# New places for gate row tiles and w_mod tiles, two loads sooner, and an uneven last zero fill

## The chip, the cores and the metric

The kernel runs on one core of a Trainium2 chip. The metric is the device time of one execution in microseconds (us). A core has five engines with instruction streams of their own: TensorE (PE), VectorE (DVE), ScalarE (ACT), GpSimd (POOL) and SyncE (SP). Sixteen transfer engines move data between HBM and the on-chip memory, and from HBM to HBM; transfers are issued from GpSimd's queue (q0 in the profile) and from SyncE's (q1).

## The reference

The kernel computes one block (adaptive layer norm, attention of one query row over a window of the cache, gated feed-forward) forward and all its gradients. What matters here:

```python
mod = (silu(c) @ w_mod).reshape(1, 6, 1, -1)
sa, ca, ga, sb, cb, gb = (mod[:, i] for i in range(6))
h = layernorm(x) * (1 + ca) + sa
x = x + ga * A(h, k_cache, v_cache, wq, wo)   # the last 4096 of 65536 cache rows, 4 heads of keys
h = layernorm(x) * (1 + cb) + sb
x = x + gb * B(h, w_gate, w_up, w_down)       # (sigmoid(h @ w_gate) * (h @ w_up)) @ w_down
return x, *vjp(grad_out)   # gradients for x, k_cache, v_cache, wq, wo, w_gate, w_up, w_down, c, w_mod
```

The gradients of the two caches have 65536 rows for each of 4 heads, and only the last 4096 are not zero. The other 61440 rows of each are written as zeros: 120 fills of 1 MB. The gradients of the weights are outer products of a column and a row, since there is one token.

## The kernel before, in words

On chip there is one large tile, `arena`, of 192 places of 1 KB in each of 128 partitions. `ar(off, size)` is a piece of it, and every weight, tile and gradient has a place there for some time. The order of all work is written out by hand. Whoever writes into a place waits until the transfer out of it, or the reading of it, is over.

The zero fills are cut from a list, `zleft`; `zero(n)` (L185) takes the next n of it and issues them on GpSimd's queue. Most are one transfer: 128 rows of 8 KB, from an on-chip tile of zeros of one byte each that are widened on the way (L209), or 32 rows from HBM to HBM (L203). Six are narrow (L191 to L199): after a reset of a cursor a transfer of 5 rows of two 256-byte pieces (L194), then one of 60 rows of two 8-KB pieces (L197). `uneven` (L171) is a third kind, for fills whose number is in `UNEVEN` (L39). `UNEVEN` is empty, so that no fill takes it. The last fill, number 119, is the one of `zero(Z_ROWS[1])` (L1332).

The last quarter of the program makes weight gradients and stores them. Its helpers:

- `dwo(u)` (L1262): 1 MB of wo's gradient, four products on VectorE, one store.
- `dw_rows(k, j, off, outer)` (L1127): one 7-KB row tile (896 KB) of the gradient of w_up (k = 0) or w_gate (k = 1), at place `off`: one product on VectorE, one store on GpSimd's queue (L1130).
- `sec(j)` (L1256): a w_mod tile. A reduction (`ttr`) in place over `w5`, a part of w_mod that is `g_t[j]` for j < 6 and a fresh load in the tile's own last quarter for j = 6 and 7; then a product into `sec_t[j]` (8 KB) and its store (L1260). `g_t[3]` lies at 54, `g_t[0]` to `g_t[5]` at 48 to 58.
- `sec_load(j)` (L1253): that load for j = 6 and 7, 256 KB each, into the last 2 KB of `sec_t[j]`, at 54 and 62.
- `dwq_tile(j)` (L1306) and `s2(j)` (L1310): tiles of 8 KB and 4 KB of the gradients of wq and of w_mod's first third, one product and one store each.
- `grad_kv` (L1289): 32 blocks for the gradient of v (into `dv_home`, places 64 to 96), later for that of k (`dk_home`, 96 to 128): a matmul for each, then ScalarE, or ScalarE and VectorE in turn, copy it out. `dv_between` and `dk_between` put `sec`, `dwq_tile` and `s2` in among the blocks. `kv_store` (L1303) stores one head, 1 MB.

Lists give the places: `sec_t` (L1246), `dwq_t` (L1248), `s2_t` (L1249). Places 0 to 16 hold `w2_t` until the product `dcs234` (L1380), 128 to 144 hold `w01_T` until `dcs01` (L1440). The name `tail` (L1464) is SyncE's queue. GpSimd's transfers use eight semaphores in turn; one is issued when the one eight before it has landed.

Of the kernel before, what the change touches and what calls it, by code (L numbers as in the profile page):

```python
# [35 lines left out]
KIB = 512  # L36
SKIP = 4
NARROW = (15, 45, 75, 93, 103, 113)
UNEVEN = ()  # L39

def spread(total, n):
# [20 lines left out]
def kernel(  # L63
# [26 lines left out]
    nc = tc.nc  # L90
# [13 lines left out]
    def ar(off, size):  # L104
        return arena[:, int(off * KIB):int((off + size) * KIB)]

    def vt(shape, name, dt=FP32):
        return pool.tile(shape, dt, name=name)
# [4 lines left out]
    ZW = 4096  # L114
    zeros = vt([P, ZW // 2], "zeros", FP8)
# [55 lines left out]
    def uneven(piece):  # L171
        parts, at = [], 0
        flat_f = piece.rearrange("i x -> (i x)").bitcast(FP32)
        nc.gpsimd.inc_swdge_sem([], [], mode="reset_dge_cursor")
        for n, x in ((7, 16), (34, 512), (6, 16), (68, 512)):
            parts.append(nc.gpsimd.dma_start(
                out=flat_f[at:at + 2 * n * x].rearrange("(t p x) -> p t x", t=2, p=n),
                in_=zeros[0:n, 0:x].rearrange("p (t x) -> p t x", t=1).broadcast_to([n, 2, x])))
            at += 2 * n * x
        left = P * ZW // 2 - at  # L180
        nc.gpsimd.dma_start(out=flat_f[at:].rearrange("(p x) -> p x", p=16),
                            in_=zero_src.rearrange("i x -> (i x)")[0:left // 2].bitcast(FP8).rearrange("(p x) -> p x", p=16))
        return parts[0]

    def zero(n, after=None, big=False):  # L185
        for _ in range(n):
            if len(zleft) <= keep[0]:
                return
            region, narrow_ = zleft.pop(0)
            first = None  # L190
            if narrow_:  # L191
                nc.gpsimd.inc_swdge_sem([], [], mode="reset_dge_cursor")
                n = nlen - ncount.pop()
                first = nc.gpsimd.dma_start(  # L194
                    out=rest[0:NS, 0:nlen * 128].rearrange("p (t x) -> p t x", t=2)[:, :, n * 64:(n + 1) * 64],
                    in_=zeros[0:NS, 0:64].rearrange("p (t x) -> p t x", t=1).broadcast_to([NS, 2, 64]))
                ins = nc.gpsimd.dma_start(  # L197
                    out=region[8:P, :].bitcast(FP32).rearrange("(t p) x -> p t x", t=2),
                    in_=zeros[0:60, :].rearrange("p (t x) -> p t x", t=1).broadcast_to([60, 2, ZW // 2]))  # L199
            elif 119 - len(zleft) in UNEVEN:  # L200
                first = ins = uneven(region)
            elif big and region.shape[0] == 1:
                ins = nc.gpsimd.dma_start(  # L203
                    out=as_rows(region, BIGP).bitcast(FP32),
                    in_=zero_src[:, 0:P * ZW // 4].rearrange("i (p x) -> (i p) x", p=BIGP).bitcast(FP8))
            else:
                if region.shape[0] == 1:
                    region = as_rows(region, P)
                ins = nc.gpsimd.dma_start(out=region.bitcast(FP32), in_=zeros[:, :])  # L209
            if after is not None:  # L210
                dep(first or ins, after)
# [32 lines left out]
    def cp(out, a):  # L244
        return nc.vector.tensor_copy(out=out, in_=a)  # L245
# [6 lines left out]
    def ttr(out, w, b, acc):  # L252
        return nc.vector.tensor_tensor_reduce(out=out, in0=w, in1=b, scale=1.0, scalar=0.0,  # L253
                                              op0=ALU.mult, op1=ALU.add, accum_out=acc)
# [13 lines left out]
    def matvec_T(blk, cols, name):  # L268
        ncol = cols.shape[2]
        ps = new_acc("mv_" + name)  # L270
        for jb in range(KD):
            for nb in range(KD):
                nc.tensor.matmul(ps[:, jb * ncol:(jb + 1) * ncol], lhsT=blk(jb, nb),
                                 rhs=cols[:, nb, :], start=(nb == 0), stop=(nb == KD - 1))
        half = ncol // 2
        v = ps[:, 0:KD * ncol].rearrange("p (j n) -> p j n", j=KD)
        res = vt([P, KD * half], name)
        r = res.rearrange("p (j n) -> p j n", j=KD)
        cp(r, v[:, :, half:ncol])
        addv(r, r, v[:, :, 0:half])  # L280
        return r
# [4 lines left out]
    def outer_dve(out, col, b):  # L286
        return ts(out, b, col, ALU.mult)
# [839 lines left out]
    def dw_rows(k, j, off, outer):  # L1127
        t = ar(off, 7)
        outer(t, h2[:, j:j + 1], dug_row[k])
        nc.gpsimd.dma_start(out=(dwu_view, dwg_view)[k][:, j, :], in_=t)  # L1130
# [112 lines left out]
    dS = ar(150, 2)  # L1243
    dq_b = ar(176, 8)
    dmod_b2 = ar(160, 4)
    sec_t = [ar(o, 8) for o in (0, 8, 152, 16, 32, 40, 48, 56)]  # L1246
    dv_home, dk_home = [ar(o, 32).rearrange("p (g x) -> p g x", g=G) for o in (64, 96)]
    dwq_t = [ar(o, 8) for o in (184, 0, 8, 152, 32, 40, 16, 48)]  # L1248
    s2_t = [ar(o, 4) for o in (164, 24, 28, 56, 60, 168, 172, 128)]  # L1249
    dcs = vt([P, KD], "dcs")  # L1250
    late = [junk[:, i * P:(i + 1) * P] for i in range(8)]

    def sec_load(j):  # L1253
        nc.gpsimd.dma_start(out=sec_t[j][:, 3 * D:4 * D], in_=wm_view[:, j, 5 * D:6 * D])

    def sec(j):  # L1256
        w5 = g_t[j] if j < 6 else sec_t[j][:, 3 * D:4 * D]
        ttr(w5, w5, dmod_b4[:, 3 * D:4 * D], dcs[:, j:j + 1])
        outer_dve(sec_t[j], cs_col[:, j:j + 1], dmod_b4)
        nc.gpsimd.dma_start(out=dwm_view[:, j, 2 * D:6 * D], in_=sec_t[j])  # L1260
# [25 lines left out]
    def kv_out(og, g):  # L1286
        return og[0, g, SKW:, :].rearrange("(p t) d -> p (t d)", t=KT)
# [15 lines left out]
    def kv_store(og, home, g, queue=nc.gpsimd):  # L1303
        queue.dma_start(out=kv_out(og, g), in_=home[:, g, :])
# [11 lines left out]
    for b in range(2):  # L1316
        do4 = new_ps("do4")
        for i in range(KD):
            for a in range(4):
# [4 lines left out]
                       in_=do4.rearrange("q (a h r) -> q a h r", a=4, h=4))  # L1324
# [51 lines left out]
    pd = b1k.bitcast(FP32)[:, 0:HQ]  # L1376
    dw_rows(1, 2, 80, outer_dve)
    zero(Z_ROWS[5])
    dw_rows(1, 3, 16, outer_dve)
    dcs234 = matvec_T(lambda jb, nb: w2_t[jb][:, nb * P:(nb + 1) * P], dh2_hl, "dcs234")  # L1380
    make_bd(DO_bd, do_bf)
    make_bd(Q_bd, q_col2[:, 0:HQ])
# [4 lines left out]
                         start=True, stop=True, tile_position=(0, 32 * tc_))  # L1387
    crow = vt([P, 1], "crow")
    cp(crow, c_ps[:, 0:1])
    sec(0)  # L1390
    dw_rows(1, 4, 32, outer_dve)
    zero(Z_ROWS[6])
    sec(1)
    dw_rows(1, 5, 88, outer_dve)
    for run in vT_unit[12:]:
        run()
    rebuild_P()
    bcast(dq_bf, HQ, dq_b, "A")
    dw_rows(1, 6, 160, outer_dve)
    zero(Z_ROWS[7])  # L1400
    dw_rows(1, 7, 40, outer_dve)
    sec(2)
    sec(3)
    sec_load(6)
    sec_load(7)
    cp(dmod_bf[:, 0:8], dh1)
    mulv(dmod_bf[:, 8:16], dh1, ln1)
    dh1_hl = hilo(dh1, KD, "dh1_hl")
# [55 lines left out]
    tail = nc.sync  # L1464
# [15 lines left out]

    grad_kv(dS, Q_bd, SCALE, dk_home, "AV", dk_between)
    for g in range(G):
        kv_store(out_2, dk_home, g, nc.gpsimd if g < 2 else tail)
    keep[0] = 0
    zero(len(zleft))
    assert not zleft and not narrow and not jobs and not bq
# [29 lines left out]
```

## Time and profile before

| what | value |
|---|---|
| three runs | 594.4, 595.35, 595.47 us; median 595.35 |
| the profiled execution | 594.57 us, of which the span (first to last instruction) is 592.8 |
| busy: PE / DVE / ACT / POOL | 430.4 / 354.9 / 248.1 / 145.9 us |
| moved by transfers | 246.58 MB in 32048 packets, mean 416 GB/s |
| HBM read, written | 79.17 MB, 185.60 MB |
| last zero fill | issued at 459.20 us |
| the eight `sec` stores | issued from 495.4 to 542.4 us |
| the two `sec_load` transfers | issued at 512.96 and 515.37 us |
| stores of the k gradient | GpSimd 571.90 and 572.42; SyncE 571.42 and 572.09 |
| the last of them landed | 591.87 us |

Times are microseconds from the start of the span. A line of the profile's table of groups names the line, the engine, the operation, what is written and read, how often; behind the first bar the busy time and the mean of one in ns, behind the second the idle time of the engine before it and what ended that. In a table of stretches each line has the stretch, its length, the busy time of each engine with the number of its instructions, the granted TensorE clock, the mean busy share of the sixteen transfer engines (it can be a little over 1, since packets overlap) and GB/s. A line of waits has who waited, for whom, the sum in us, how often, and the longest. The chain of waits follows the work that ended last back in time: in the last 93 us half of it is stores out of `arena` (50.2%).

### The profile page before, as it was taken

What the parts mean: (1) busy time and instruction counts of PE and PEld (TensorE: products, weight loads), DVE (VectorE), ACT (ScalarE), POOL (GpSimd) and SP (SyncE); (2) the same over time, 40 slices, a digit from 0 to 9 for tenths busy, and PEclk for the clock granted to TensorE, in tenths of its full rate; (3) what the DMA queues carried; (4) which work ended last, traced back from release to release, by engine and by line L of the source; (5) the groups of instructions that cost most, each with busy time, mean ns of one, the idle gap of its engine ahead of it and who ended that gap; (6) DMA issues with size and microseconds to landing.
All of it is one profiled execution on the core that took longest, in us unless ns stands there. A gap on an engine that the chain in (4) does not pass through costs nothing.

```text
span 592.8 us, 10216 instructions
## 1 busy us (share of the span) xinstructions
PE 430.4 (73%) x4196; PEld 245.4 (41%) x4196; DVE 354.9 (60%) x647; ACT 248.1 (42%) x398; POOL 145.9 (25%) x251
## 2 busy tenths in 40 slices
PE   3997789999999999997977757776655446084510
PEld 2784433333334545543544545555442445013100
DVE  3665679988930102039373866887986869536750
ACT  2579511554540103411224635665671455093410
POOL 3112213122122212122222331323222433213100
PEclk9998689999999999998998757777785658555555
DMA  8999999999999999999999999999999999999997
GB/s 348 421 420 421 422 465 426 425 422 429 426 404 461 417 438 421 410 420 435 427 395 409 418 412 407 397 408 410 423 422 426 424 425 425 422 408 418 414 417 302
DMA packets 32048, 246.58 MB, mean 416 GB/s; under 512 B 4782, under 2 KB 4782, under 8 KB 16689
## 3 DMA queue, kind: packets, MB, share of 16 engines
q0 software_dynamic: 27008, 226.51, 94.8%
q1 hardware_dynamic: 4944, 19.41, 9.2%
q8 instruction: 33, 0.54, 0.4%
q14 instruction: 15, 0.11, 0.0%
q10 hardware_dynamic: 48, 0.01, 0.0%
HBM read 79.17 MB, written 185.60 MB: 447 GB/s over the span
## 4 chain that ended last, share of the span: by engine, by line
PE 35%; DMA 33%; DVE 16%; ACT 6%; issue 6%; POOL 1%; ACTq 0%; POOLq 0%; DVEq 0%
DMA out_dram<-arena 12%; PE b_ps L796 11%; PE n_ps L737 9%; DMA arena<-in_w_mod_dram 6%; DMA arena<-in_B_w_gate_dram 5%; DVE arena L249 4%; PE t_ps L685 4%; DMA out_dram<-out_dram 3%; DVE arena L253 3%; DMA arena<-in_B_w_up_dram 3%; ACT arena L524 2%; DVE scr L253 2%; DVE arena L236 2%; DMA arena<-in_B_w_down_dram 2%; PE tp_k L503 1%
## 5 line engine op out<-in xcount | busy, mean ns | idle before, releaser
L796 PE MATMUL b_ps<-arena 128*128 128x512 bf16 x512 | 118.6, 384 | 1.1 <-ACT arena L940 1.1
L940 ACT COPY arena<-tp_side 128x1024 bf16<-128x1024 bf16 x62 | 60.9, 1017 | 53.0 <-PE tp_side L939 52.2
L236 DVE TENSOR_TENSOR arena<-arena 128x2048 bf16<-128x2048 bf16 x64 | 77.7, 1224 | 8.8 <-PE n_ps L737 5.1
L796 PEld LDWEIGHTS <-arena 128*128 128x128 bf16 x512 | 49.0, 99 | 58.0 <-issue 5.4
L737 PE MATMUL n_ps<-arena 128*128 128x512 bf16 x256 | 67.7, 389 | 3.4 <-DVE arena L236 2.9
L203 POOL DMA_DIRECT2D out_dram<-out_dram x72 | 35.7, 496 | 127.4 <-PE n_ps L737 57.3
L939 PE MATMUL tp_side<-ident_bf,arena 128*128 128x128 bf16 x496 | 50.6, 270 | 9.6 <-DVE arena L236 5.3
L939 PEld LDWEIGHTS <-arena 128*128 128x128 bf16 x496 | 42.0, 124 | 18.4 <-issue 9.1
L1295 PE MATMUL ps_kv<-arena 32*128 32x512 bf16 x64 | 26.6, 581 | 27.6 <-DVE arena L257 11.7
L693 ACT CAST arena<-t_ps 128x512 bf16<-128x512 f32 x56 | 28.9, 598 | 39.9 <-PE t_ps L685 39.9
L1299 ACT ACTIVATE arena<-ps_kv 128x512 bf16<-128x512 f32 x48 | 25.0, 714 | 39.6 <-PE ps_kv L1295 20.5
L253 DVE CUSTOM_DVE_ANT_0 arena<-arena,scr 128x1024 bf16<-128x1024 bf16 x35 | 40.8, 1218 | 0.2
L737 PEld LDWEIGHTS <-arena 128*128 128x128 bf16 x256 | 21.4, 99 | 35.6 <-issue 19.4
L209 POOL DMA_DIRECT2D out_dram<-zeros x42 | 23.2, 554 | 52.4 <-DVE rows_all L236 22.9
L253 DVE CUSTOM_DVE_ANT_0 scr<-arena,b1k 128x1024 bf16<-128x1024 bf16 x28 | 34.2, 1222 | 2.8 <-DMA arena<-in_B_w_down_dram 2.4
L245 DVE CAST arena<-b_ps 128x512 bf16<-128x512 f32 x6 | 4.1, 692 | 50.2 <-PE b_ps L796 50.2
L249 DVE TENSOR_SCALAR arena<-arena,h 128x3584 bf16<-128x3584 bf16 (+1 forms) x24 | 28.3, 1191 | 7.9 <-DMA out_dram<-arena 7.8
L685 PE MATMUL t_ps<-arena 128*32 128x512 bf16 x256 | 24.1, 399 | 2.8 <-ACT arena L760 2.8
L1295 PEld LDWEIGHTS <-arena 32*128 32x128 bf16 x64 | 6.8, 112 | 46.2 <-issue 45.4
L249 DVE TENSOR_SCALAR arena<-arena,cs_col 128x4096 bf16<-128x4096 bf16 (+1 forms) x16 | 16.0, 1015 | 15.2 <-DMA out_dram<-arena 15.2
L524 ACT COPY arena<-tp_wq 128x1024 bf16<-128x1024 bf16 x23 | 21.4, 1066 | 7.3 <-PE tp_wq L522 7.3
L1077 ACT COPY arena<-tp_ug 128x1024 bf16<-128x1024 bf16 x21 | 20.5, 1008 | 6.7 <-PE tp_ug L1076 6.7
(326 smaller groups left out, 660.3 us busy)
## 6 DMA issues: line engine op xcount, KB each, us to landing
out_dram<-zeros POOLq DMA_DIRECT2D x42, 1024.0 KB, 12.6
out_dram<-arena POOLq DMA_DIRECT2D x35, 1024.0 KB, 15.0
out_dram<-arena POOLq DMA_DIRECT2D x16, 896.0 KB, 17.3
arena<-in_A_wq_dram POOLq DMA_DIRECT2D x8, 1024.0 KB, 21.0
arena<-in_A_wo_dram POOLq DMA_DIRECT2D x8, 1024.0 KB, 13.3
arena<-in_w_mod_dram POOLq DMA_DIRECT2D x7, 1024.0 KB, 19.0
arena<-in_B_w_up_dram POOLq DMA_DIRECT2D x14, 512.0 KB, 11.5
arena<-in_B_w_gate_dram POOLq DMA_DIRECT2D x14, 512.0 KB, 14.5
```

The lines of the kernel that those rows point to most:

```text
L203: ins = nc.gpsimd.dma_start(out=as_rows(region, BIGP).bitcast(FP32), in_=zero_src[:, 0:P * ZW // 4].rearrange("i (p x) -> (i p) x", p=BIGP ...
L236: return nc.vector.tensor_tensor(out=out, in0=a, in1=b, op=op)
L249: return nc.vector.tensor_scalar(out=out, in0=a, scalar1=s1, scalar2=None, op0=op0)
L253: return nc.vector.tensor_tensor_reduce(out=out, in0=w, in1=b, scale=1.0, scalar=0.0, op0=ALU.mult, op1=ALU.add, accum_out=acc)
L524: nc.scalar.copy(out=blk, in_=tp[:, :])
L685: nc.tensor.matmul(ps[32 * hh:32 * hh + 32, :].rearrange("p (j m) -> p j m", j=4), lhsT=N_sb[:, h * P + a:(h + 1) * P - 3 + a:4], rhs=a4[: ...
L693: nc.scalar.copy(out=o, in_=v)
L737: mm = nc.tensor.matmul(nbank[k][:, :], lhsT=k_nat[:, g, t_ * DH:(t_ + 1) * DH], rhs=vp[:, t_ % 2, 4 * k:4 * k + 4, :].rearrange("p h d -> ...
L796: mm = nc.tensor.matmul(bbank[p][k][:, :], lhsT=a4[:, p, h, :], rhs=wo_t[u][:, a, k * 512:(k + 1) * 512], start=(i == 0 and a == 0), stop= ...
L939: nc.tensor.transpose(tp[:, i * P:(i + 1) * P], blk[:, i * P:(i + 1) * P], ident_bf[:, :])
L940: nc.scalar.copy(out=blk if dst is None else dst, in_=tp[:, :])
L1295: nc.tensor.matmul(ps[:, :], lhsT=rows[r, t8 * P:(t8 + 1) * P], rhs=bd[r, :], start=True, stop=True, tile_position=(32 * tc_, 0))
```

## The change

- `UNEVEN` holds 119, so that the last fill is written by `uneven`; and `uneven` has other transfers: after the reset, 7 rows of two 64-byte pieces, 2 rows of twelve 8-KB pieces, 6 rows of two 64-byte pieces, 4 rows of twelve 8-KB pieces; the rest of the 1 MB (457,088 bytes) goes as 16 rows from HBM to HBM. That is five transfers and a reset for one transfer.
- `sec_t`: tile 0 from 0 to 8, tile 1 from 8 to 168, tile 3 from 16 to 0. `sec(3)` goes to the front, and both `sec_load` right behind it; `sec(0)` follows the row tile (1, 4), `sec(1)` and `sec(2)` follow (1, 7).
- The row tiles of w_gate: (1, 3) from 16 to 88, (1, 5) from 88 to 40, (1, 7) from 40 to 16.
- `dwq_t`: tile 5 from 40 to 16, tile 6 from 16 to 40. `s2_t`: tiles 3, 4, 5 from 56, 60, 168 to 132, 136, 140.
- `kv_store` of the k gradient's head 1 goes from GpSimd's queue to SyncE's.

```diff
-UNEVEN = ()
+UNEVEN = (119,)
...
-        for n, x in ((7, 16), (34, 512), (6, 16), (68, 512)):
+        for n, t, x in ((7, 2, 16), (2, 12, ZW // 2), (6, 2, 16), (4, 12, ZW // 2)):
             parts.append(nc.gpsimd.dma_start(
-                out=flat_f[at:at + 2 * n * x].rearrange("(t p x) -> p t x", t=2, p=n),
-                in_=zeros[0:n, 0:x].rearrange("p (t x) -> p t x", t=1).broadcast_to([n, 2, x])))
-            at += 2 * n * x
+                out=flat_f[at:at + t * n * x].rearrange("(t p x) -> p t x", t=t, p=n),
+                in_=zeros[0:n, 0:x].rearrange("p (t x) -> p t x", t=1).broadcast_to([n, t, x])))
+            at += t * n * x
...
-    sec_t = [ar(o, 8) for o in (0, 8, 152, 16, 32, 40, 48, 56)]
+    sec_t = [ar(o, 8) for o in (8, 168, 152, 0, 32, 40, 48, 56)]
...
-    dwq_t = [ar(o, 8) for o in (184, 0, 8, 152, 32, 40, 16, 48)]
-    s2_t = [ar(o, 4) for o in (164, 24, 28, 56, 60, 168, 172, 128)]
+    dwq_t = [ar(o, 8) for o in (184, 0, 8, 152, 32, 16, 40, 48)]
+    s2_t = [ar(o, 4) for o in (164, 24, 28, 132, 136, 140, 172, 128)]
...
-    dw_rows(1, 3, 16, outer_dve)
+    dw_rows(1, 3, 88, outer_dve)
...
-    sec(0)
+    sec(3)
+    sec_load(6)
+    sec_load(7)
     dw_rows(1, 4, 32, outer_dve)
     zero(Z_ROWS[6])
-    sec(1)
-    dw_rows(1, 5, 88, outer_dve)
+    sec(0)
+    dw_rows(1, 5, 40, outer_dve)
...
-    dw_rows(1, 7, 40, outer_dve)
+    dw_rows(1, 7, 16, outer_dve)
+    sec(1)
     sec(2)
-    sec(3)
-    sec_load(6)
-    sec_load(7)
...
-        kv_store(out_2, dk_home, g, nc.gpsimd if g < 2 else tail)
+        kv_store(out_2, dk_home, g, nc.gpsimd if g < 1 else tail)
```

## The prediction

> **What bounds the kernel now.** I read the page's slices first, then its table of queues, then stretches of the last fifth, then what VectorE and ScalarE wait for there.
>
> ```profile
> DMA  8999999999999999999999999999999999999997
> GB/s 348 421 420 421 422 465 426 425 422 429 426 404 461 417 438 421 410 420 435 427 395 409 418 412 407 397 408 410 423 422 426 424 425 425 422 408 418 414 417 302
> ...
> q0 software_dynamic: 27008, 226.51, 94.8%
> q1 hardware_dynamic: 4944, 19.41, 9.2%
> ```
>
> The transfer engines are full from the second slice to the last but one: the kernel moves 246.58 MB and ends when that is done. Only the last slice (302 GB/s) has room. The stretches, whose last two columns are the transfer engines' busy share and GB/s, show where:
>
> ```profile
> 440.00:480.00 40.00, 17.45 (x198) 11.60 (x197) 31.47 (x78) 14.14 (x15) 14.46 (x20) 0.63 1.06 425
> 480.00:520.00 40.00, 18.30 (x303) 14.36 (x304) 27.49 (x46) 16.03 (x26) 11.68 (x18) 0.67 1.01 423
> 520.00:530.00 10.00, 9.61 (x20) 1.98 (x20) 2.48 (x2) 10.00 (x22) 2.09 (x3) 0.50 1.01 398
> 530.00:560.00 30.00, 14.41 (x111) 6.87 (x110) 19.94 (x45) 13.29 (x26) 7.35 (x12) 0.50 1.01 418
> ...
> 577.00:586.00 9.00, 0.00 (x0) 0.00 (x0) 0.00 (x0) 0.00 (x0) 0.00 (x0) 0.50 1.01 419
> 586.00:588.00 2.00, 0.00 (x0) 0.00 (x0) 0.00 (x0) 0.00 (x0) 0.00 (x0) 0.50 0.91 379
> 588.00:590.00 2.00, 0.00 (x0) 0.00 (x0) 0.00 (x0) 0.00 (x0) 0.00 (x0) 0.50 0.36 152
> 590.00:592.80 2.80, 0.00 (x0) 0.00 (x0) 0.00 (x0) 0.00 (x0) 0.00 (x0) 0.50 0.06 23
> ```
>
> Every compute engine is done by 572, and the sixteen transfer engines run dry one after another from 586. What moves after 586 is 2x379 + 2x152 + 2.8x23 = 1126 KB, which sixteen engines ending together would move in 2.7 us at 419 GB/s. The last store lands at 591.9, so perfect balance is worth 591.9 - 588.7 less some 0.4 us between a last byte and its semaphore step: 2.8 us. That is the most that balance can give.
>
> VectorE and ScalarE wait for places whose old stores have not landed:
>
> ```profile
> DVE arena L249 <- DMA out_dram<-arena: 15.2, 4, 6.2
> ...
> DVE arena L253 <- DMA arena<-in_w_mod_dram: 4.8, 1, 4.8
> ...
> ACT arena L1299 <- DMA out_dram<-arena: 19.0, 1, 19.0
> ```
>
> These 39 us are long, but the transfer engines have a queue through all of them (share 1.01). They set the chain of waits, not the amount left to move.
>
> **Who ends late.** A transfer adds sixteen steps to its semaphore, one an engine, and the trace keeps them. The last fill (issued 459.20) has 467.0, 467.1, 467.1, 467.2, 467.5, 467.6 | 468.4 | 469.5, 469.5, 469.5, 469.6 | 470.9, 471.0, 471.0, 471.1, 471.2: six engines about 2 us ahead of the mean, one between, nine behind. The last store has 586.6, 586.9, 588.3, 588.4, 588.4, 588.5, 588.6, 588.7, 589.0, 589.2, 589.5, 590.0, 590.2, 590.3, 591.7, 591.9. So the picture of 459 lasts to the end: nothing later rebalances the engines.
>
> **The fill, step by step.** A plain fill gives each engine eight 8-KB pieces. From the trace's packets such a piece takes 0.306 us start to start, so 2.45 us. The new one: six engines write twelve pieces (3.67 us), then all sixteen share the other 457 KB, 28.6 KB each. Packets of 64 KB between HBM places take 2.431 us, so this is 1.06 us. Six engines have 4.73 (2.28 more than now), ten have 1.06 (1.39 less). If the six are the six early ones, they end at 588.5 + 2.28 = 590.8 and the ten at 591.9 - 1.39 = 590.5: the end comes 1.07 us sooner.
>
> Two costs come off that. The new pieces begin 896 bytes into the region, and the trace has no 8-KB piece so placed. The nearest is the 2,880-byte one of the remainder fill, which took 127 to 171 ns where the 8-KB rate gives 108 to 111: 16 to 63 ns over. Bounds for twelve pieces: nothing to 0.76 us on the six. I take the low row, 0.19, since that excess may be one packet's fixed cost. Four more transfers with their own semaphore step (9 ns each) and some 64-byte pieces (below the 31 to 38 ns of the 256-byte ones) cost each engine under 0.1 us; I take 0.05.
>
> Which six engines? The trace does not name engines. Read from the code, each transfer of n rows takes n places from a cursor that was reset: 7 rows places 0 to 6, 2 rows 7 and 8, 6 rows 9 to 14, 4 rows 15, 0, 1 and 2. The narrow fill of 424.7 uses the same device with 5 rows, and five engines wrote its small pieces, at 430.8, 431.2, 431.3, 432.2 and 432.6; three of these five are among the early six. So places 0, 1 and 2 are early as far as the trace can say; of 7, 8 and 15 it says nothing. The Trainium skill ("DMA: Bandwidth & Descriptors", "Why a DMA increments its semaphore by 16 and not by 1") states that a GpSimd transfer on k < 16 engines takes k consecutive ones from a round-robin cursor; the five writers of the narrow fill agree with that.
>
> GpSimd issues five transfers where it issued one: 4 x 0.55 to 0.8, some 2.5 us. It has eight semaphores in turn and issues only when the transfer eight back has landed. With four places taken, dwo(2) issues when 464.2 is reached (the landing of the fill of 449.6), not 460.2; dwo(0) at 466.6, dwo(4) at 468.8. The least loaded engine reaches dwo(2) at about 467.0, so the cover is 3 us and the cost nothing; were the cover gone, each microsecond of delay would be one at the end. VectorE does not wait for GpSimd here; the stores stand in the same order in the queues and land no later.
>
> **The moves.** No product is added: each gate tile keeps a 1.22 us reduction and a 1.28 us product, each 7-KB row tile 1.15 us, each its store (0.53 to 1.1 us of GpSimd). sec(3) goes ahead of three of the row tiles and sec(0), with its 1-MB store; the two w_mod loads follow it (0.55 and 0.86 us of GpSimd; 256 KB each, 0.6 us of the queue), in front of some ten stores, which land about 1.2 us later than by their old turn. What goes: the wait of 6.2 us at 504 (sec(3) for the row tile at 16), of 5.4 us at 518 (sec(5) for the row tile at 40), 4.8 at 526 (the load), 3.4 at 556 (s2(3) for sec(7)'s store at 56), and most of ScalarE's 19.0: its first write into 64..96 waits for the row tile at 88, stored at 501.9 and landed at 519.4; now that is stored at 493 and lands near 510. What is late next: sec(4) for the row tile at 32, whose store comes after sec(3) and both loads, so it waits to about 515.5, as now (514.83), with dwq_tile(0), the dv stage and GpSimd's stores behind it. sec(1) at 168 needs dwo(1), landed 505.9, and VectorE comes there at about 506. The places 128 to 144 of s2 need only TensorE's reading of w01_T, over by 539. So the last dk column should be done near 557 to 562, not 571.4, and the last stores be issued that much sooner. All of it lies under the full queue: 0.09 us at most, the one spot (535 to 536) where the engines' share fell from 16.2 to 14.7 engines.
>
> kv_store(out_2, 1) moves from GpSimd (0.53 us) to SyncE (0.6 to 1.2 us), behind store 2's place in line; the queue holds 5 us of work then, so nothing. With SyncE's stores earlier, both queues run together longer. Together they gave 419 GB/s (577 to 586), alone 425 (440 to 480): 1.4% of perhaps 15 us more, 0.2 us of loss, against the chance that the 398 GB/s at 520 to 530 (0.6 us lost against 423) does not come back. I take zero for the two, with -1.1 (that, and 530 to 560 at 425 rather than 418: 0.5) and +0.2 as bounds.
>
> **Sum.** -1.07 + 0.19 + 0.05 - 0.09 = -0.9 us: 594.57 in the profiled execution (span 592.8 and 1.8 around it) becomes 593.7. The median of the runs shown, 595.35, lies 0.8 above that execution, so I predict 594.4.
>
> **Rivals.** *More than balance* (593.3): the earlier loads no longer meet the stores of 520 to 530, and both terms above come in, 1.1 us more. For it: the dip sits exactly where loads stand among stores. Against: the same 512 KB must still be read.
>
> *Nothing* (595.0): the six become the late ones. With 63 ns over for each of twelve pieces they end at 588.5 + 2.28 + 0.76 = 591.6, 0.3 sooner.
>
> *Slower* (597.6): one of the six is not early but one of the late. An engine that now steps at 591.9 ends at 594.2, and the kernel 2.3 us later. It decides from any picked engine whose last step is now beyond 589.6; five of sixteen are. For it: only three of the six are tied to early engines by a row. Against: exactly six are early, and they stand apart by 0.8 us from the seventh. A sentence from the Trainium skill speaks for this rival: "DMA: Bandwidth & Descriptors", "Latency and other measured facts", says that engines 7 and 15 are usually slower than the rest. By it two picked engines would be among the late, and the time this 597.6; no row here names an engine 7 or 15, and the 8-KB packets after 588 all last 309 to 312 ns.
>
> **Chances.** Forecast 0.50 (two fifths of it beyond 0.2%), more than balance 0.25, nothing 0.06, slower 0.19. This kernel's runs spread by 0.2%, about 1.2 us, so less than that can't be told from no change. Faster: 0.20 + 0.25 = 0.45; within: 0.30 + 0.06 = 0.36; slower: 0.19. The forecast's own range is 593.6 to 595.0. The range for 8 in 10 takes in the second case with its bound and the run's spread (592.7), and above it half of the slower one: 597.0.
>
> **What would show it.** The last store's sixteen steps within 3 us instead of 5.3, the highest within 2 us of their mean; the share of 586 to 588 back near 1. The fill's five transfers at 459 with six steps far behind the other ten's. VectorE's four waits and ScalarE's 19 us gone and the last stores issued ten microseconds sooner, with the end moved by only one: that would confirm that compute is not the bound. Two late steps further out than 591.9 would say that the six were chosen wrongly; a share below 1 between 465 and 480 that the eight semaphores starved the queue.

## The result, and the profile after

The change made the kernel slower, by 0.5%: 597.91 us (median of 6; 597.19 to 598.75) against 594.93 (6 runs of the kernel before beside them; 594.23 to 595.47), a ratio of 1.0054, 95% interval 1.004 to 1.0068. The profiled execution took 598.36 us, its span 596.3, against 594.57 and 592.8.

The slices and queues of the changed kernel's page:

```profile
GB/s 351 422 418 419 425 457 424 426 428 444 423 395 452 418 440 432 423 404 448 418 413 381 421 403 403 401 407 412 424 424 427 381 406 406 391 424 409 413 415 312
...
q0 software_dynamic: 27264, 225.46, 94.3%
q1 hardware_dynamic: 5088, 20.46, 9.7%
```

The same 246.58 MB move, 1 MB of it by the other queue. The slices show where it goes more slowly: number 32 (462 to 477 us) has 381 GB/s where it had 424, and the three behind it have 406, 406 and 391 where they had 425, 425 and 422. The last stretches, columns as before (the last two are the transfer engines' share and GB/s); first two stretches of the kernel before, then the changed kernel's:

```profile
468.00:472.00 4.00, 0.00 (x0) 0.00 (x0) 3.73 (x8) 1.15 (x2) 1.51 (x3) 0.89 1.05 426
472.00:476.00 4.00, 0.00 (x0) 0.00 (x0) 1.15 (x1) 0.00 (x0) 1.15 (x2) 0.50 1.01 428
```

```profile
464.00:468.00 4.00, 2.24 (x20) 1.83 (x18) 4.00 (x10) 3.43 (x4) 1.15 (x2) 0.72 1.06 405
468.00:472.00 4.00, 0.00 (x0) 0.00 (x0) 3.60 (x8) 0.00 (x0) 4.00 (x2) 0.71 0.86 340
472.00:476.00 4.00, 0.00 (x0) 0.00 (x0) 1.58 (x2) 0.00 (x0) 4.00 (x7) 0.50 0.98 391
476.00:480.00 4.00, 0.57 (x15) 0.49 (x16) 2.94 (x3) 2.18 (x3) 2.75 (x3) 0.50 1.00 387
480.00:520.00 40.00, 23.00 (x314) 15.44 (x312) 24.02 (x43) 21.48 (x38) 11.23 (x16) 0.67 1.01 400
520.00:530.00 10.00, 6.61 (x14) 1.19 (x12) 9.06 (x10) 9.41 (x20) 3.47 (x5) 0.50 1.02 427
530.00:560.00 30.00, 16.34 (x117) 7.90 (x117) 24.41 (x53) 10.80 (x20) 9.44 (x12) 0.50 1.01 412
...
586.00:588.00 2.00, 0.00 (x0) 0.00 (x0) 0.00 (x0) 0.00 (x0) 0.00 (x0) 0.50 0.99 410
588.00:590.00 2.00, 0.00 (x0) 0.00 (x0) 0.00 (x0) 0.00 (x0) 0.00 (x0) 0.50 1.02 426
590.00:592.00 2.00, 0.00 (x0) 0.00 (x0) 0.00 (x0) 0.00 (x0) 0.00 (x0) 0.50 0.79 332
592.00:596.30 4.30, 0.00 (x0) 0.00 (x0) 0.00 (x0) 0.00 (x0) 0.00 (x0) 0.50 0.22 93
```

Two things are to be seen. The end is steeper, as meant: the share stays near 1 to 590 and then falls within 5 us. But 468 to 472 has a share of 0.86: the engines ran dry in the middle, and then for 40 us they are busy (1.01) and move 400 GB/s where they moved 423. Why they ran dry is in GpSimd's and VectorE's timelines (start, length, how many). GpSimd's first, before and after the change, then VectorE's after it:

```profile
460.18 0.62 POOL L1265 DMA_DIRECT2D out_dram<-arena  x1 [0.17 <-issue]
461.76 0.71 POOL L1265 DMA_DIRECT2D out_dram<-arena  x1 [0.97 <-DVE do_bf L245]
463.44 1.41 POOL L1265 DMA_DIRECT2D out_dram<-arena  x1 [0.97 <-DVE arena L249]
```

```profile
459.10 3.29 POOL L176 DMA_DIRECT2D out_dram<-zeros  x4
462.38 0.77 POOL L181 DMA_DIRECT2D out_dram<-out_dram  x1
464.66 0.59 POOL L1265 DMA_DIRECT2D out_dram<-arena  x1 [1.51 <-DVE arena L249]
467.44 5.85 POOL L1265 DMA_DIRECT2D out_dram<-arena  x4 [2.19 <-DVE arena L249]
```

```profile
467.30 1.67 DVE L249 TENSOR_SCALAR arena<-scr,kb_col 128x1024 bf16<-128x1024 bf16 x4
468.88 1.14 DVE L249 TENSOR_SCALAR arena<-arena,h 128x3584 bf16<-128x3584 bf16 x1
469.94 1.66 DVE L249 TENSOR_SCALAR arena<-scr,kb_col 128x1024 bf16<-128x1024 bf16 x4
473.13 1.15 DVE L249 TENSOR_SCALAR arena<-arena,h 128x3584 bf16<-128x3584 bf16 x1 [1.53 <-DMA out_dram<-arena]
```

Of the four issues from 467.44 on, the first, dwo(0)'s, lasts 4.29 us, the others 0.52 each. It ends at 471.72, 0.12 us after VectorE's products stop at 471.60. What is issued and not yet moved, from the issue times and the packets, would last 6.3 us at 465 and 4.0 at 470; in the kernel before it was 11.1 and 15.8. An issue counts here from its start, and 2.5 of the 4.0 us are dwo(0)'s store, whose issue was not over: only 1.6 us could move.

The span is 3.5 us longer. The sixteen steps of the last store come 3.9 us later on the mean (592.99 against 589.12); the latest of them stands 1.6 us behind that mean where it stood 2.8 behind, so that part is 1.2 us better, as much as forecast, though not by the fill, as the part on the prediction shows; and the span ends 1.8 us behind the latest step where it ended 0.9 behind. An estimate from GB/s shows where the 3.9 us go: 464 to 480 moved 381 GB/s where it moved 425 (1.7 us of work at 423), 480 to 520 moved 400 where it moved 423 (2.2), 520 to 530 gave 0.7 back (427 for 398), and from 530 to 586 0.5 was lost: 3.7 in all.

The moves did what they say. ScalarE's 19.0 us for a store are gone (it waits 11.0 us for VectorE in their place), VectorE's longest wait for a store is 4.5 us instead of 6.2 (their sum is the same 15.2, over 486 to 575), and the k stores are issued at 563.7 to 569.3 instead of 571.4 to 572.4:

```profile
DVE arena L249 <- DMA out_dram<-arena: 15.2, 5, 4.5
...
ACT arena L1299 <- PE ps_kv L1295: 17.0, 11, 9.1
ACT arena L1299 <- DVE dh_hl L245: 11.0, 1, 11.0
```

### The profile page after: what moved, and what is told of

It reads as the page before. It is cut to its first block, busy times and chain, and to the rows that moved or that the text cites. A ratio compares the mean times of both kernels' runs of the same rounds, so it can differ in the third digit from the quotient of the medians.

```text
span 596.3 us, 10223 instructions
## 1 busy us (share of the span) xinstructions
PE 427.6 (72%) x4196; PEld 242.9 (41%) x4196; DVE 354.6 (59%) x647; ACT 248.0 (42%) x398; POOL 154.5 (26%) x254
## 2 busy tenths in 40 slices
DMA packets 32447, 246.58 MB, mean 413 GB/s; under 512 B 5221, under 2 KB 5221, under 8 KB 17128
## 4 chain that ended last, share of the span: by engine, by line
PE 33%; DMA 30%; DVE 20%; issue 6%; ACT 5%; POOL 1%; ACTq 0%; DVEq 0%; POOLq 0%
DMA out_dram<-arena 10%; PE b_ps L796 10%; DMA out_dram<-out_dram 9%; PE n_ps L737 9%; DVE arena L249 7%; DMA arena<-in_B_w_gate_dram 5%; DVE arena L253 4%; PE t_ps L685 3%; DMA arena<-in_B_w_up_dram 2%; DVE scr L253 2%; ACT arena L524 2%; DMA out_dram<-zeros 2%; DVE arena L236 2%; PE tp_k L503 1%; PE w_ps L466 1%
## 5 line engine op out<-in xcount | busy, mean ns | idle before, releaser
L796 PEld LDWEIGHTS <-arena 128*128 128x128 bf16 x512 | 49.0, 100 | 58.0 <-issue 5.4
L939 PE MATMUL tp_side<-ident_bf,arena 128*128 128x128 bf16 x496 | 48.4, 262 | 11.5 <-DVE arena L236 5.8
L939 PEld LDWEIGHTS <-arena 128*128 128x128 bf16 x496 | 40.1, 119 | 20.3 <-issue 10.7
L1295 PE MATMUL ps_kv<-arena 32*128 32x512 bf16 x64 | 25.6, 582 | 17.2 <-DVE arena L257 11.1
L737 PEld LDWEIGHTS <-arena 128*128 128x128 bf16 x256 | 21.4, 99 | 35.6 <-issue 19.2
L965 POOL DMA_DIRECT2D arena<-in_B_w_up_dram x14 | 10.7, 766 | 42.3 <-DVE dh2acc L253 24.6
```

Source lines behind the costliest of these rows:

```text
L737: mm = nc.tensor.matmul(nbank[k][:, :], lhsT=k_nat[:, g, t_ * DH:(t_ + 1) * DH], rhs=vp[:, t_ % 2, 4 * k:4 * k + 4, :].rearrange("p h d -> ...
L796: mm = nc.tensor.matmul(bbank[p][k][:, :], lhsT=a4[:, p, h, :], rhs=wo_t[u][:, a, k * 512:(k + 1) * 512], start=(i == 0 and a == 0), stop= ...
L939: nc.tensor.transpose(tp[:, i * P:(i + 1) * P], blk[:, i * P:(i + 1) * P], ident_bf[:, :])
L1295: nc.tensor.matmul(ps[:, :], lhsT=rows[r, t8 * P:(t8 + 1) * P], rhs=bd[r, :], start=True, stop=True, tile_position=(32 * tc_, 0))
```

## The experiments

Each ran beside the kernel before, whose median was 594.33 to 594.74 us in the five sets.

| kernel | median, us | ratio to before, 95% interval |
|---|---|---|
| before + fill only | 597.01 | 1.0048 (1.0029 to 1.0067) |
| moves only | 594.9 | 1.001 (0.9997 to 1.0022) |
| changed, five even transfers | 598.33 | 1.0072 (1.0056 to 1.0088) |
| changed, two row tiles on ScalarE | 597.48 | 1.0071 (1.0046 to 1.0095) |
| changed, dwo(3)'s products three times | 602.47 | 1.0137 (1.0121 to 1.0152) |
| fill one place earlier, uneven | 596.24 | 1.0029 (1.0019 to 1.0039) |
| the same, even | 595.46 | 1.0015 (1.0005 to 1.0025) |
| the same, other six engines | 596.15 | 1.003 (1.0018 to 1.0043) |
| uneven fill last of all | 603.39 | 1.0149 (1.0135 to 1.0163) |
| moves only, late stores on GpSimd | 598.31 | 1.0065 (1.0052 to 1.0077) |
| uneven earlier, late stores on GpSimd | 600.15 | 1.0094 (1.008 to 1.0107) |
| before, late stores on GpSimd | 599.03 | 1.0073 (1.0059 to 1.0087) |
| moves only, k store back | 595.68 | 1.0028 (1.0014 to 1.0043) |
| moves only, tail stores on GpSimd, two k stores on SyncE | 598.76 | 1.007 (1.0053 to 1.0088) |
| changed, k store back | 598.37 | 1.0069 (1.0054 to 1.0083) |
| moves only, one w_mod store on GpSimd | 595.1 | 1.0017 (1.0 to 1.0033) |
| moves only, one wq store on GpSimd | 595.09 | 1.0012 (0.9999 to 1.0024) |
| changed, one w_mod store on GpSimd | 597.44 | 1.005 (1.0035 to 1.0066) |

One of the nine runs with two row tiles on ScalarE took 603.29 us, the others 596.85 to 598.17; it raises that ratio, and the medians alone give 1.0048. In four kernels some runs lie apart from the rest: fill only, three of six (597.7 to 598.0, the rest 596.1 to 596.3); moves only with the k store back, three of twelve (597.8 to 598.3, the rest up to 595.9); moves only with one w_mod store on GpSimd, four of twelve (597.2 to 597.3, the rest up to 595.4); with one wq store, one of twelve (597.73). None of those apart was profiled, so their cause is not shown.

### Which part costs it: fill or moves

Fill alone: the kernel before with `UNEVEN = (119,)` and the new shapes of `uneven`. Moves alone:

```diff
-UNEVEN = (119,)
+UNEVEN = ()
```

> The kernel before with only the last fill changed to five transfers (uneven pieces); no tile has a new place and no load goes sooner. Theory A (the fill's four extra issues on GpSimd starve the transfer queue): all of the loss comes with the fill, 2.5 to 3.5 us over the kernel before, some 597.5 to 598.5; one of GpSimd's issues for dwo near 467 lasts over 2 us, and the transfer engines' share of some stretch of 4 us between 464 and 478 falls below 1. Rival B (the moves cost the time: the two loads ahead of ten stores, the new places): 594 to 595, that is the same or faster than before, with the share at 1.03 or more there.

> The changed kernel with its last fill put back to one plain transfer; the new places, the sooner loads and the store on the other queue stay. Theory A: the loss goes with the fill, within 1 us of the kernel before (594 to 595.5); no GpSimd issue between 459 and 475 lasts over 1.5 us, and the six early engines keep their lead to the end (the last store's sixteen steps spread over 5 us as before). Rival B: the loss stays, about 597.5 to 598.5.

The fill alone is 2.4 us slower, the moves alone can't be told from before. So the fill is what costs the time. The moves alone have no dry stretch:

```profile
468.00:472.00 4.00, 0.49 (x5) 0.27 (x3) 4.00 (x10) 1.50 (x2) 1.84 (x4) 0.93 1.05 424
472.00:476.00 4.00, 0.00 (x0) 0.00 (x0) 1.42 (x2) 0.00 (x0) 1.21 (x2) 0.50 1.02 430
```

Two signs missed. The moves alone have an issue of 3.09 us too, at 461.8, and it costs nothing: 11 us of work are queued there. And the fill alone is slower although in its profile no issue behind the fill lasts over 1.21 us and the share from 464 to 480 does not fall below 1.01. That profile is of one of the three lower runs, 596.06 us, so it accounts for 1.5 of the 2.4 us, and the upper three may have starved. But its last step comes 1.46 us later than before (593.33 against 591.87), so starvation is not the only way in which the fill costs time.

### Many transfers, or uneven ones

```diff
-        for n, t, x in ((7, 2, 16), (2, 12, ZW // 2), (6, 2, 16), (4, 12, ZW // 2)):
+        for n, t, x in ((7, 2, 16), (16, 2, ZW // 2), (6, 2, 16), (16, 2, ZW // 2)):
```

> The changed kernel with its last fill in five transfers and with the same cursor reset and four small 64-byte pieces, but the 8-KB pieces shared evenly: 64 of them, four for each of the sixteen engines, and the rest evenly. Theory A (it is the number of issues, not who writes what): as slow as the changed kernel within 1 us (597 to 599), with a GpSimd issue of over 2 us near 467 and a share below 1 behind it. Rival C (the wrong engines were picked for the twelve pieces, or pieces at odd places cost more): the loss goes, as with the plain fill (594 to 595.5).

As slow as the changed kernel, with an issue of 4.65 us at 467.2 and 278 GB/s at 468 to 472: at this place five transfers cost the time, whoever writes what. This profile starved, as the changed kernel's did.

### What holds the issue back

The two row tiles on ScalarE, and in the other direction dwo(3)'s products written three times over (twice more than needed):

```diff
-    dw_rows(0, 3, 16, outer_dve)
+    dw_rows(0, 3, 16, outer_act)
...
-    dw_rows(0, 4, 32, outer_dve)
+    dw_rows(0, 4, 32, outer_act)
```

```diff
-    def dwo(u):
-        for a in range(4):
+    def dwo(u, times=1):
+        for a in [0, 1, 2, 3] * times:
...
-    dwo(3)
+    dwo(3, 3)
```

> The changed kernel with the two row tiles of 467 to 471.6 (dw_rows(0,3) and dw_rows(0,4)) written by ScalarE instead of VectorE, so that VectorE has nothing to write in that stretch. Theory T2 (GpSimd can't finish issuing a transfer while VectorE's products run): the issue of 4.29 us at 467.4 shortens by 2 us or more, dwo(4) issues by about 469.5 instead of 471.7, the stretch of 468 to 476 moves more than 364 GB/s, and the kernel gains 1 to 2.5 us on the changed one. Rivals T1 and T3 (the eight semaphores in turn, or a full ring of descriptors, hold the issue back): the issue still ends at 471 or later and the time stays within 0.5 us of the changed kernel.

> The changed kernel with the four products of dwo(3) written three times over, so that VectorE is at work without a break to about 474.9 instead of 471.6. Theory T2: the issue that begins near 467.4 is held to within 0.15 us behind the end of some VectorE product, most likely the last one: up to 7.5 us instead of 4.29; the stretch of 468 to 476 moves less than 364 GB/s, and the kernel is 1 to 3.5 us slower than the changed one. Rivals T1 and T3 (the semaphores in turn, a full ring): the issue ends at 471.7 as before and the time stays within 0.7 us.

With ScalarE, VectorE's products stop at 469.82 and the issue ends at 469.93, after 2.69 us instead of 4.29; 468 to 476 moves 404 and 418 GB/s. With more products an issue begins at 469.43 and ends at 478.30, 0.12 us after VectorE's last product (478.18): 8.87 us. GpSimd's timeline and the stretches of that run:

```profile
467.31 0.80 POOL L1265 DMA_DIRECT2D out_dram<-arena  x1 [1.82 <-DMA out_dram<-arena]
469.43 9.92 POOL L1265 DMA_DIRECT2D out_dram<-arena  x3 [1.32 <-DVE arena L249]
```

```profile
472.00:476.00 4.00, 0.00 (x0) 0.00 (x0) 4.00 (x10) 0.00 (x0) 4.00 (x1) 0.50 0.42 178
476.00:480.00 4.00, 0.37 (x8) 0.29 (x8) 2.18 (x3) 1.78 (x2) 4.00 (x5) 0.50 0.32 131
```

The cause of the long issue is shown in both directions; semaphores or a full ring would have kept its end at 471.7. The time gained on ScalarE is only 0.4 us, though (597.48 against 597.91, in different sets), and 0.1 when each is held against the kernel before of its own set (2.88 us above it against 2.98), where 1 to 2.5 were expected: again most of the fill's cost stays without the starvation.

### The fill where no product runs

The fill one place earlier (449.6): uneven, even, and with the twelve pieces for places 9 to 14.

```diff
-UNEVEN = (119,)
+UNEVEN = (118,)
```

```diff
-        for n, t, x in ((7, 2, 16), (2, 12, ZW // 2), (6, 2, 16), (4, 12, ZW // 2)):
+        for n, t, x in ((9, 2, 16), (6, 12, ZW // 2)):
```

> The changed kernel with the same five transfers one fill earlier (issued near 449.6, while VectorE has little to write) and the last fill plain. Theory A: no GpSimd issue lasts over 2 us, no stretch between 464 and 480 falls below 1.0, and the loss of the changed kernel goes: at most 1 us over the kernel with the moves alone. Theory L (engines that stand close together move less: behind the fill the six are level with the others, and the queue gives 408 to 418 GB/s where spread engines give 423): no starvation, but the rate of 480 to 512 stays at 408 to 418 and 1 to 2 us of the loss stays, 595.5 to 597. Rival S (starvation explains all): 423 GB/s there, and the balance pays: 593.5 to 594.5.

> As the kernel with the uneven fill one place earlier, but the 8-KB pieces shared evenly by all sixteen engines: five issues, no balance. Theory L: the engines stay as far apart as before (steps of one transfer spread over 4 us), so 480 to 512 moves 421 GB/s or more and the time is that of the moves alone, 594 to 595.5. Rival: the number of transfers or their small pieces cost by themselves, so that it is as slow as the uneven one at this place.

> The fill one place earlier, with the twelve 8-KB pieces given to the engines of places 9 to 14, none of which is among the six of the change (nine small pieces go ahead). Theory: places 0, 1, 2, 7, 8 and 15 are the early ones, so these six are late ones, fall back by another 2.3 us, and the sixteen steps of a transfer spread over 6 us or more. By theory L the rate of 476 to 512 is then 423 GB/s or more, as spread engines give, and the loss comes at the end: last steps 2 us later than with the moves alone, 596 to 597.5. Rival (any uneven fill lowers the rate): below 418 GB/s there.

By the medians the even one costs 0.6 us over the moves alone, which the intervals do not tell from nothing; the uneven one costs 1.3, and 0.8 over the even one in the same set. Nothing runs dry at 464 to 480 (418 to 430 GB/s in the uneven one), though one sign missed: an issue lasts 2.83 us there, at 461.9. The first line is of the uneven, the second of the even one:

```profile
480.00:512.00 32.00, 18.48 (x303) 14.65 (x301) 23.52 (x41) 16.96 (x28) 9.86 (x14) 0.66 1.01 414
```

```profile
480.00:512.00 32.00, 18.20 (x305) 14.46 (x306) 23.45 (x41) 17.25 (x29) 9.44 (x14) 0.71 1.01 419
```

The standard deviation of a transfer's sixteen steps at 480 to 504 is 0.5 to 0.8 us in the uneven one, 1.5 to 1.6 in the even one, and 3.0 with the other six (their steps spread over 8 us). So the places that the change picks are the early ones, and the fill does level the engines. But with level engines less is moved here, and the number of transfers is not why: the even one has as many.

### Levelling the very end

```diff
-Z_ROWS = (1, 1, 0, 0, 0, 0, 0, 0)
+Z_ROWS = (1, 0, 0, 0, 0, 0, 0, 0)
```

> The changed kernel with its uneven fill issued as the very last transfer (behind the last store of GpSimd, near 566, where no VectorE product runs and some 18 us of work are queued) instead of at 459. Theory: no stall, no starvation, the engines stay spread to the end as with the moves alone (423 GB/s at 476 to 512), and only the last microseconds are made level: if the same six engines are still the early ones, 1 us faster than the moves alone, 593 to 594.5. If others have become the early ones by 580, the six end late and it is 1 to 2 us slower, 595.5 to 597. Rival: with 1 MB less in the queue behind 459 it runs dry there, a share below 1 between 464 and 476 and 597 or more.

Much worse. Nothing ran dry at 464 to 476 (424 to 428 GB/s), but the fill's last three transfers are issued only at 564.89, 568.76 and 571.61, each behind the transfer eight before it, and one of the four engines of the second wide transfer steps at 595.7 when the next one is at 591.1: by then one of the picked engines was the latest of all. The last transfer is now GpSimd's, and the span ends 4.1 us behind its step (1.8 in the moves alone), for the reason that the next section shows.

### One queue at the end

```diff
-    tail = nc.sync
+    tail = nc.gpsimd
```

> The kernel with the moves alone, but the late stores that SyncE issues (the tail stores and three dk stores) issued by GpSimd instead, so that from 545 on one queue is at work where two were. Theory Q (two queues at once lower the rate from 426 to 414 GB/s and push the engines apart, from a standard deviation of 1.5 us between the sixteen steps to 2.7): 530 to 577 moves 422 to 427 GB/s, the deviation stays below 1.8 us to the end, and the kernel is 0.7 to 2 us faster, 593 to 594.2. Rival: the rate of 414 belongs to these stores, not to the queues, or GpSimd's eight semaphores hold the stores back: no gain or a loss, 594.5 or more.

> The kernel with the moves and the uneven fill one place earlier (no starvation there), and its late stores on GpSimd's queue too. Theory Q: the level that the fill makes (steps 0.5 to 1.0 us around their mean at 500 to 530) lasts to the end, the last sixteen steps lie within 3.5 us instead of 4.6, and it is 1 to 2.5 us faster than with SyncE's queue (594 to 595.2 against 596.2). Rival (the engines come apart by themselves, whatever the queue): the spread at the end is 4 us or more again and the time stays above 595.5.

> The kernel before with its late stores on GpSimd's queue instead of SyncE's, nothing else changed. Theory Q: 552 to 577 moves 422 to 427 GB/s instead of 414, and the time falls by 0.4 to 1.5 us, to 593 to 594.2. Rival: same or slower, since without the moves only 6 to 10 us of work are queued there and GpSimd's issues come in turn.

All slower, and the rate does not rise (407 to 410 GB/s over 544 to 576; 414 in the kernel before, 416 in the moves alone). A part of the theory holds: with one queue the deviation of the steps stays at 1.1 to 1.4 us to the end in the first and the third, and their last step lands at 591.0 and 591.4, 0.4 and 0.5 sooner; in the second it grows from 0.5 to 2.0. With two queues GpSimd's transfers deviate by 1.9 to 2.8 between 560 and 572, but the last store of all by 1.4 to 1.5 only, hardly more than with one. But the span ends 4.7 us behind the last step: GpSimd's closing DRAIN ends 3.6 to 3.8 us after its own last step.

### What lies behind the last step

In the changed kernel the span ends 1.8 us after the last step, in the kernel before 0.9. SyncE's instructions at the end (start, end, what it waits for), after and before:

```
after   594.58 594.61 S[100], S[115]      before  589.44 589.47 S[107], S[101]
        595.03 595.06 S[102], S[114]              591.89 591.91 S[108], S[118]
        595.12 595.14 S[103], S[113]              591.95 591.96 DRAIN
        ... five more, 0.06 apart
        595.50 595.50 DRAIN
```

SyncE waits for its semaphores in a fixed order, and with one transfer more on its queue the last store has the first of them, and seven waits come behind it, 0.84 us. The eight profiles of kernels whose last store has S[100] all end 1.8 us behind the last step. Undone: the k store back, on the moves alone, on the changed kernel, and with the tail stores moved as well; then the k store stays, and one other store leaves SyncE (the 0.5 MB of `s2(2)`, or the 1 MB of `dwq_tile(6)`). Shown are the edits of the k store and of `s2(2)`.

```diff
-        kv_store(out_2, dk_home, g, nc.gpsimd if g < 1 else tail)
+        kv_store(out_2, dk_home, g, nc.gpsimd if g < 2 else tail)
```

```diff
-            s2(2, tail)
+            s2(2)
```

> The kernel with the moves alone, with the dk store that the change gave to SyncE back on GpSimd; nothing else. Theory W (SyncE's closing waits go through its semaphores in a fixed order; with one transfer more on SyncE the last store has the first of them, and eight waits come behind it, 0.84 us): the last wait is again that of the last store, the span ends 0.9 us behind its last step instead of 1.7, and the time falls by 0.5 to 1.2 us, to 593.7 to 594.4, which is also 0.2 to 0.9 below the kernel before. Rival: that tail was an accident of one profile, and the time stays at 594.9.

> The changed kernel whole, with only that dk store back on GpSimd. Theory W: 0.5 to 1.2 us less than the changed kernel (597.9), 596.7 to 597.4: the end is 0.9 us behind the last step. Rival: no change.

> As the kernel with the dk store back on GpSimd, and the eight tail stores (two weight-gradient columns of rows and six of w_mod) on GpSimd's queue too, so that SyncE issues the last two dk stores alone. Theory Q2 (two queues at once only push the engines apart; what made one queue slow was GpSimd's drain, 3.6 us behind its own last landing): the sixteen steps of the last store within 5 us, the drain over before the last step, and 0.3 to 0.8 us faster than the kernel with the store back alone (593 to 593.9). Rival: GpSimd's stores come later by their eight semaphores in turn and the drain ends last: 595 or more.

> The kernel with the moves alone; the dk store stays on SyncE, as the change has it, but one store of a w_mod column (s2(2), 0.5 MB) goes to GpSimd instead, so that SyncE again issues as many transfers as before and the last store has the last of SyncE's semaphores. Theory W2 (two tails compete: GpSimd's drain ends 3.3 to 3.6 us behind its own last landing, and SyncE's waits cost 0.84 us when the last store's semaphore comes first): the drain ends by 589, the span ends 0.9 us behind the last step, and the time is 0.4 to 1.2 us below the moves alone, 593.5 to 594.4. Rival: 594.9 or more, since the store of the column lands late on GpSimd's queue or the end moves with it.

> As the run with one w_mod column's store on GpSimd, but the transfer that changes queue is one of 1 MB (the store of dwq_tile(6)), so that the two queues hold more alike. Theory W2: GpSimd's last landing near 586, its drain over by 590, the end 0.9 us behind the last step; 0.4 to 1.5 us below the moves alone (593.2 to 594.4). Rival: the drain ends last, 594.9 or more.

> The changed kernel whole, with only the store of that w_mod column on GpSimd. Theory W2: 0.4 to 1.2 us below the changed kernel, 596.7 to 597.5, the end 0.9 us behind the last step. Rival: no change (597.9).

None is faster than the kernel before. The wait order is mended in the five whose last store is SyncE's, and DRAIN takes its place: with the k store back on the moves alone the last step comes at 590.46, 1.4 us sooner than before, but GpSimd's last packet ends at 588.62 and its DRAIN at 592.19. One 0.5-MB store more on GpSimd's queue moves its last packet from 583.96 to 588.66, which I had not expected. In the fourteenth kernel of the table GpSimd itself lands last and DRAIN adds 3.6 us behind it.

## Why the prediction was wrong

The end is set by the latest engine, so here is the landing of its step (us) at five transfers, in two pairs that differ in the fill alone:

| latest engine at | moves only | changed | moves only, w_mod store on GpSimd | changed, the same |
|---|---|---|---|---|
| dwo(2), first behind the fill | 473.70 | 473.03 | 473.73 | 473.19 |
| dwo(3) | 492.74 | 494.37 | 492.76 | 492.20 |
| row tile (1, 3) | 510.99 | 513.32 | 510.25 | 510.65 |
| second w_mod load | 514.62 | 517.38 | 514.20 | 516.35 |
| last step | 591.39 | 594.56 | 591.47 | 594.14 |

In the first pair the fill gains 0.67 us, starvation takes 2.30 (473.70 - 473.03 + 494.37 - 492.74), the way to the row tile 0.70, the store of sec(3) with the loads 0.43, the rest 0.41: 3.17 later. In the second pair the long issue (2.52 us) starves nobody for long; the gain of 0.5 lasts to dwo(3), then 0.96 goes by the row tile, 1.75 at sec(3) and its loads, and 0.52 behind: 2.67 later. Three more pairs that differ in the fill alone go the same way: k store back (0.74 sooner at dwo(2), 3.36 later at the last step), fill only against the kernel before (1.00 sooner, 1.46 later), and uneven against even at 449 (0.65 sooner, 0.73 later). The kernels with the fill have a longest issue of 2.5, 1.2 and 2.8 us there, and the share from 464 to 480 stays at 1.00 or more in all three. With the products on ScalarE it is alike: 0.79 sooner than the moves alone at dwo(2), 0.21 at dwo(3), 2.04 later at the last step. So one loss stands where the other did, and that is why this run gained so little.

By the prediction's steps:

- *What bounds the kernel*: right. The moves alone end the last product ten microseconds sooner (560.7 for 571.4) and change nothing (1.001).
- *Which six engines*: right. The picked ones are early, places 9 to 14 are not. The Trainium skill ("DMA: Bandwidth & Descriptors", "Latency and other measured facts") says that engines 7 and 15 are usually slower; if places 7 and 15 are these, no run here agrees, since a fill for them levels the steps (from 1.5 to 0.8 us and less).
- *The size of the gain*: -1.07 was expected, and behind the fill at 119 the latest engine is 0.5 to 1.0 us sooner (0.67 in the changed kernel's profile). The sign named for success, the last store's steps within 3 us and the highest within 2 of their mean, came in the changed kernel (3.1 and 1.6), but also with five even transfers (3.5 and 1.9), and not where the uneven fill at 119 or 449 left no dry stretch (3.7 to 5.9 and 2.3 to 3.5). So it is the dry stretch that levelled them, and not the fill.
- *GpSimd's five issues, "the cover is 3 us and the cost nothing"*: this step failed. I counted the issues at 0.55 to 0.8 us each, and the cover up to dwo(2) alone. For dwo(2) it holds: issued at 464.66, reached by the first engine at 467.04. One store later it does not: the first engine is done with dwo(2) at 469.57, and dwo(0)'s issue ends at 471.72. Without a VectorE product beside it an issue lasts at most 0.64 us (558 of them, from 430 us on, in all profiles); beside products it can last until one of them ends, and all 435 issues over 0.7 us end 0.09 to 0.14 us behind a product. The fill puts little into five of eight places in line, so that 6.3 us are queued where there were 11, and then an issue of 4.29 us decides. The Trainium skill has the rule, and I did not weigh it: "SBUF — State Buffer", section "SBUF: two separate sides", says that GpSimd can't write the descriptors of its transfers while VectorE holds the port that they share, until some 115 ns after VectorE's operation ends. The traces agree, with 0.12 us; that nine products in a row can pass without letting it in (sixteen in the run with more products) is what they add.
- *"Nothing later rebalances the engines"*: failed, with the rate that the sum took for granted. It had no term for what the transfers behind the fill move, and 480 to 520 lost 2.2 us by it. And the level does not last: with the uneven fill of 449 the steps deviate by 0.4 us ahead of the store of sec(3), by 0.9 behind it and by 2.4 to 2.8 in GpSimd's transfers from 560 on, as in the moves alone (2.4 to 2.8). The last step is 592.4 there, against 591.7 with even pieces. Whether it is the two queues at once that set the engines apart from 555 on is not settled: with one queue and this fill they come apart too (2.0).
- *"The stores land no later"*: failed. dwo(0) lands 1.4 us later on the mean, the row tile (1, 3) 3.0.
- *The k store on SyncE, "so nothing"*: failed by 0.8 us at the end, through the order of SyncE's waits. Its place on GpSimd is no better, because of DRAIN.
- *The rivals*: the slower one gave 597.6 and the time came near it, but for another reason: it blamed a late engine among the six, and the two uneven fills of 449, with these six and with six others, refute that. The rival of more than balance had the dip at 520 to 530 right, but in the moves alone its 425 GB/s there (398 before) go with 415 at 500 to 512, and the mean of the last steps comes 0.2 us sooner. The sign named for starvation (a share below 1 between 465 and 480) is what came.

What stays open: why level engines move less. It is seen in all five pairs, and with five even transfers too, which left the engines level by their dry stretch; but no run takes the two loads away, and that the level itself is the cause is argued from the agreement of the profiles, not shown. What the traces show is in the last section. Nor is it shown how often the changed kernel starves: of four profiles with its fill at 119 and its products on VectorE, one has an issue over 4 us, two have 2.5, one (the fill alone) none over 1.21.

## What to carry to other kernels

Before a transfer is cut into several, count what each of the pieces holds in the queue: a fixed number of transfers in flight is a fixed number of bytes only while they are large, and a queue that is short meets the next issue held up by VectorE. Levelling transfer engines early is worth little if later work sets them apart again; look at the steps of a late transfer before working on an early one. And look at what stands behind the last byte on each queue, since which queue carries the last store can be worth more than its bytes.

## What the runs showed of the hardware

- Level engines are slower at a store followed by loads. The 1-MB store of the w_mod tile that stands ahead of the two loads takes, from the mean step before it to its own, 3.05 to 3.48 us in the nine profiles whose steps deviate by 0.4 to 1.1 us there, and 2.60 to 2.99 in the eleven whose steps deviate by 1.5 or more; elsewhere a 1-MB store takes some 2.45. In the 15 us around it, 8-KB packets of over 500 ns (309 is usual) number 31 to 51 in the nine, 9 to 24 in the eleven. Why is not shown.
- Where no load is near, the most level engines lose too: from 480 to 490 the changed kernel, with a deviation of 0.2 to 0.5 us, falls back by some 0.4 us behind the one before, the moves alone by nothing; the uneven fill of 449, with 0.7 to 0.8 us there, loses nothing.
- GpSimd's DRAIN at the end ends 3.2 to 3.8 us behind its last landing; SyncE's closing waits take 0.06 to 0.45 us each, 0.84 for the seven behind the first.
